# Adding six key row tiles on GpSimd ahead of the key-sum matmuls, and rearranging the mask work around the normaliser products

## The chip, the cores and the metric

The kernel runs on one core of a Trainium2 chip. The metric is the device time of one execution in microseconds (us), as the median of several runs; lower is better. One core has five engines that run their own instruction streams in order: TensorE (PE in the profile, with its weight loads listed as PEld), VectorE (DVE), ScalarE (ACT), GpSimd (POOL) and SyncE (SP), which here only issues DMA transfers. They meet at semaphores.

## The reference, cut to what matters

The program is the forward and backward pass of one block: layer norm, linear attention with 32 heads of 20 columns, a residual, a second layer norm and a gated MLP. S is 2048 rows, D is 640 columns. Only the forward attention matters here:

```python
phi = lambda t: jnp.where(t > 0, t + 1, jnp.exp(t)) + 1e-6
pq, pk = phi(q), phi(k)
kv = jnp.einsum("bhsd,bhse->bhde", pk, v)
z = jnp.einsum("bhsd->bhd", pk)                 # key sums over all 2048 rows
num = jnp.einsum("bhqd,bhde->bhqe", pq, kv)
den = jnp.einsum("bhqd,bhd->bhq", pq, z)[..., None] + 1e-6
o = num / den
```

`z` is the vector of 640 key sums. For every query row, `den` needs the products `pq * z` added up inside each head.

## The kernel before, in words

Rows are split in 16 tiles of 128 (`t` = 0 to 15), columns in 5 chunks of 128 (`m` or `c` = 0 to 4). The schedule is manual: each engine carries out its instructions in the order in which the Python code issues them, so an instruction that waits holds up everything behind it on its engine.

**The key loop (lines 515 to 558).** For each row tile, TensorE multiplies the normalised rows by the key weights (`p1_mm`, line 266), ScalarE takes exp and relu of the result (lines 293 and 294, groups `mq` and `rq`), and VectorE finishes phi in two instructions (line 297, a tensor_scalar on `mq`, and line 298, an add). They write `pk_all[:, t, :]`, bf16. VectorE's part of tile t is held back and issued in the next round of the loop (`held`, `phi_rest`). TensorE also accumulates `M = pk^T x` with `m_part` (line 416), chunk by chunk of the key columns, as rows become available. Four query tiles are computed inside the loop, the others after it. In rounds 11 to 15 the loop clears a chunk of `bd` (line 551) and calls `make_mask(t - 11)`.

**The masks (lines 198 to 206).** `make_mask(m)` builds a 0/1 pattern that keeps the columns of a row's own head. VectorE sets the chunk to one (line 201), then GpSimd runs two affine selects on it (lines 203 and 205). The masks are read by `masked` (line 211), which clears the off-head entries of `kvT_block(m)`; the result `bd` feeds `f2_wT` (line 690).

**The key sums.** For chunks 0 and 1 a column of ones appended to `x` gives them along with M (`m_end`, line 425). For chunks 2, 3 and 4 `z_late` (line 329) issues 16 row tiles times 3 chunks = 48 matmuls with a one-column right side (line 333), each with its own 128x128 weight load. ScalarE copies the three columns into `Z` (line 335), `z_diag` (line 327) puts each chunk on the diagonal of a matrix `dz`, and `z_rows` (line 339) multiplies a matrix of ones by `dz` (line 343), which spreads the key sums over all 128 partitions. ScalarE copies them to `Zb` (line 346).

**The normaliser.** `r_prod(t)` multiplies a query tile by `Zb` in two halves of 320 columns, on GpSimd for t < 8 (line 358). `r_row(t)` on VectorE sums inside the heads (line 365), adds the small constant (368), inverts (369) and scales the query tile in place (372); `r_T(t)` has the scaled tile transposed by a DMA. Two buffers for each parity of t hold the products, so the product of tile t+2 waits for the sum of tile t.

**Order behind the loop (lines 573 to 624).** The order is written out by hand: query tile 4, the rest of M's chunks 0 and 1, `z_late`, ten row tiles of M's chunk 2, `z_rows`, then query tiles, products, heads and more of M in turn. After it come `q_late`, `kv3`, `f2_wT` (line 868), whose outputs are transposed to `Wp` by DMA, and the attention output `f2_at` (line 642).

Of the kernel before, what the change touches and what calls it, by code (L numbers as in the profile page):

```python
# [9 lines left out]
P = 128  # L10
BF16 = mybir.dt.bfloat16
F32 = mybir.dt.float32
ALU = mybir.AluOpType
# [5 lines left out]
S, D, H, F = 2048, 640, 32, 1728  # L19
DH = D // H  # L20
ST, DT = S // P, D // P
# [34 lines left out]
def kernel(  # L56
# [19 lines left out]
    V, A, T, G, SY = nc.vector, nc.scalar, nc.tensor, nc.gpsimd, nc.sync  # L76
# [42 lines left out]
    ones = cp.tile([P, P], BF16, name="ones")  # L119
# [6 lines left out]
    rden = cp.tile([P, ST, H], F32, name="rden")  # L126
    bd = cp.tile([P, DT, D], BF16, name="bd")
    Zb = cp.tile([P, D], BF16, name="Zb")
# [67 lines left out]
    mask = cp.tile([P, DT, M_MAX, DH], BF16, name="mask")  # L196

    def make_mask(m):
        a, b = M_H[m]
        v = mask[:, m, 0:b - a, :]  # L200
        V.memset(v, 1.0)

        G.affine_select(out=v, in_=v, pattern=[[-DH, b - a], [0, DH]], compare_op=ALU.is_ge, fill=0.0,
                        base=m * P - a * DH, channel_multiplier=1)
        G.affine_select(out=v, in_=v, pattern=[[DH, b - a], [0, DH]], compare_op=ALU.is_gt, fill=0.0,
                        base=a * DH + DH - m * P, channel_multiplier=-1)
# [27 lines left out]
    pk_all = p1.tile([P, ST, D], BF16, name="pk_all", tag="pk")  # L234
# [16 lines left out]
    def p1_tr(t, parts=((0, DT),)):  # L251
        xn = x_sb[:, t, :]
        for a, b in parts:
            tr = ps.tile([P, DT, P], BF16, name="tr", bufs=2)
            for c in range(a, b):
                T.transpose(tr[:, c, :], xn[:, c * P:(c + 1) * P], ident[:])

            A.copy(out=pqT[:, a:b, t * P:(t + 1) * P], in_=tr[:, a:b, :])
# [13 lines left out]
    def p1_mm(t, n0, between=None, halves=None):  # L272
        acc = p1_acc() if halves is None else None
        for j in range(2):
            p1_half(acc[:, j, 0:HD] if halves is None else halves[j][:, 0:HD], t, n0 + j * HD)
            if j == 0 and between is not None:
                between()
        return acc
# [6 lines left out]
    def phi_tiles():  # L285
        return [p1.tile([P, D], BF16, name=n, bufs=3) for n in ("mq", "rq")]

    def phi(acc, dst, t, parts=None):

        mq, rq = parts or phi_tiles()  # L290
        if parts is None:
            kw = dict(scale=ln1.rs[:, t:t + 1]) if t < RAW else {}
            A.activation(two(mq[:]), acc[:, :, 0:HD], AF.Exp, **kw)
            A.activation(two(rq[:]), acc[:, :, 0:HD], AF.Relu, **kw)

        def rest():
            V.tensor_scalar(out=mq[:], in0=mq[:], scalar1=1.0, scalar2=1e-6, op0=ALU.min, op1=ALU.add)
            V.tensor_tensor(out=dst, in0=mq[:], in1=rq[:], op=ALU.add)
        held.append(rest)

    def phi_rest(keep=0):
        while len(held) > keep:
            held.pop(0)()

    pqs = {}
    hx = ph.tile([P, FT * W], BF16, name="hx", tag="H1")[:, 0:11 * D].rearrange("p (t n) -> p t n", n=D)
    pq6, mbs = hx[:, 0:6, :], hx[:, 6:10, :]

    def q_home(t):
        if t < 4 or 8 <= t < 10:  # L310
            pqs[t] = pq6[:, t if t < 4 else t - 4, :]
        elif t < 8:
            pqs[t] = pf.tile([P, D], BF16, name="pql", bufs=4)[:]
        else:
            pqs[t] = pkx[0][:, DT + t - 10, :]
# [3 lines left out]
    def q_tile(t):  # L319
        q_home(t)  # L320
        phi(p1_mm(t, 0), pqs[t], t)
# [3 lines left out]
    def z_diag(m):  # L325
        dz[m] = hx[:, 10, m * P:(m + 1) * P]
        V.tensor_scalar(out=dz[m], in0=ident[:], scalar1=Z[:, m:m + 1], scalar2=None, op0=ALU.mult)

    def z_late(ms, acc):

        for t in range(ST):
            for i, m in enumerate(ms):
                T.matmul(acc[:, i:i + 1], lhsT=pk_all[:, t, m * P:(m + 1) * P], rhs=ones[:, 0:1],
                         start=(t == 0 and i == 0), stop=(t == ST - 1), skip_group_check=True)
        A.copy(out=Z[:, ms[0]:ms[-1] + 1], in_=acc[:, 0:len(ms)])
        for m in ms:
            z_diag(m)
# [12 lines left out]
    def r_prod(t):  # L350
        for j in range(2):
            js = slice(j * HD, (j + 1) * HD)
            if t < 8:
                pr[t, j] = (p1.tile([P, HD], F32, name="pr", bufs=2) if t % 2 else
                            pf.tile([P, HD], F32, name="pr", tag="h2", bufs=2))[:]
            else:
                pr[t, j] = ps.tile([P, 512], F32, name="prp", tag="at", bufs=2)[:, 0:HD]
            (G if t < 8 else V).tensor_tensor(out=pr[t, j], in0=pqs[t][:, js], in1=Zb[:, js], op=ALU.mult)
# [16 lines left out]
    def r_T(t):  # L375
        dmaT(out=pqT[:, :, t * P:(t + 1) * P], in_=pqs[t])
# [34 lines left out]
    def m_part(m, tiles, js=(0, 1)):  # L411
        if m not in macc:
            macc[m] = [ps.tile([P, 512], F32, name="macc", tag=("m", "tr")[m % 2], bufs=2) for _ in range(2)]
        for t, j in [(t, j) for t in tiles for j in js]:
            n = HD + (m < 2) * j
            T.matmul(macc[m][j][:, 0:n], lhsT=pk_all[:, t, m * P:(m + 1) * P],  # L416
                     rhs=x_ext[:, t, j * HD:j * HD + n], start=(t == 0), stop=(t == ST - 1))
# [97 lines left out]
    for t in range(ST):  # L515
        first = None
        if t < RAW:
            first = phi_tiles()
            kh = [ps.tile([P, 512], F32, name="k0", tag="m", bufs=2) for _ in range(2)]

            def act(i, j):
                A.activation(first[i][:, j * HD:(j + 1) * HD], kh[j][:, 0:HD], (AF.Exp, AF.Relu)[i],
                             scale=ln1.rs[:, t:t + 1])

            def between():
                act(0, 0)
                p1_tr(t + 1)
                act(1, 0)
            k = p1_mm(t, D, between, kh)
            act(0, 1)  # L530
            act(1, 1)
        else:
            k = p1_mm(t, D, (lambda: p1_tr(t + 1)) if t + 1 < XT_DMA else None)
        steps = v_steps.get(t, (R,) * len(held))
        for step in steps:
            if step is R:
                held.pop(0)()
            elif step[0] in V_OPS:
                V_OPS[step[0]](step[1])
        phi(k, pk_all[:, t, :], t, first)  # L540
        for when in ("A", "B", "L"):
            for step in steps:
                if step is not R and step[0] == when:
                    p1_norm(step[1])
            if when == "A" and t in QT:
                q_tile(QT.index(t))
        if 3 <= t < 7:
            ghh_chunk(t - 3, ps.tile([P, 512], F32, name="gp", tag="m", bufs=2))
        m_part(0, M0.get(t, ()))
        if t >= 11:  # L550
            V.memset(bd[:, t - 11, :], 0.0)
            make_mask(t - 11)
        if t >= 9:
            m_part(1, [2 * (t - 9), 2 * (t - 9) + 1])
        for f, *n in outs.get(t, ()):
            f(*n)
        if t in trickle:
            trickle[t]()
# [10 lines left out]
    def r_head(t):  # L569
        r_row(t)  # L570
        r_T(t)

    q_tile(4)
    m_part(0, (13, 14, 15))
    m_end(0)
# [5 lines left out]
    for go in w13[4:]:  # L581
        go()
    z_late((2, 3, 4), big())
    m_part(2, range(10))
    z_rows(((0, 1), (2, 3, 4)), ps.tile([P, 2, 512], F32, name="bigx", tag="big", bufs=2))
    r_prod(0)
    q_tile(5)
    r_prod(1)
    m_part(2, range(10, ST))
# [1 line left out]
    dmaG(out=m_v[:, 0, :], in_=mbs[:, 0, :])  # L591
    r_head(0)
    r_prod(2)
    phi_rest()
    m_part(3, range(5))
    q_tile(6)
    r_head(1)
    r_prod(3)
    phi_rest()
    m_part(3, range(5, 11))  # L600
    q_tile(7)
    kvT_block(0, big())
    r_row(2)
    r_prod(4)
    phi_rest()
    m_part(3, range(11, ST))
    m_end(3)
# [2 lines left out]
    dmaG(out=m_v[:, 1:4, :], in_=mbs[:, 1:4, :])  # L610
    r_head(3)
    r_prod(5)
    m_part(4, range(5))
    q_tile(8)
    kvT_block(1, big())
# [301 lines left out]
    for c in range(SC):  # L917
# [9 lines left out]
        for fc in range(FT):  # L927
# [8 lines left out]
            if c == 0 and fc in (5, 7, 9, 11):  # L936
                a, b = {5: (0, 3), 7: (3, 6), 9: (6, 10), 11: (10, 13)}[fc]
# [12 lines left out]
            if c == SC - 1 and fc in (1, 2, 5, 6):  # L950
                i = (1, 2, 5, 6).index(fc)
# [66 lines left out]
    for fc in range(FT - 1):  # L1018
        b, i = divmod(fc, 4)
        if fc == FT - 2:  # L1020
            gw2_tail()
        acc = ps.tile([P, 2, 512], F32, name="gw", bufs=4)
        for j in range(2):
            for t in range(ST):
                T.matmul(acc[:, j, 0:HD], lhsT=hb[b][:, t, i * P:(i + 1) * P], rhs=g2[:, t, j * HD:(j + 1) * HD],  # L1025
                         start=(t == 0), stop=(t == ST - 1))
# [200 lines left out]
    a, b = ST - 1, ST - 2  # L1227
# [90 lines left out]
    for m, (a, b) in enumerate(M_H):  # L1318
        n = (b - a) * DH
        acc = ps.tile([P, 512], F32, name="gkvT", tag="dkv", bufs=3)  # L1320
        for c in range(DT):
            T.matmul(acc[:, 0:n], lhsT=woT[:, c, m * P:(m + 1) * P], rhs=QT[:, c, a * DH:b * DH], start=(c == 0),
                     stop=(c == DT - 1))
# [38 lines left out]
    acc = d_acc()  # L1362
    for m in range(DT):
        T.matmul(acc[:, m // 4, m % 4 * P:(m % 4 + 1) * P], lhsT=ones[:], rhs=gzd[:, m, :], start=(m % 4 == 0),
                 stop=True, skip_group_check=True)
# [3 lines left out]
    for t in range(ST):  # L1369
        c, i = divmod(t, TPC)  # L1370
        u = t // 2
        acc = d_acc()
        for j in range(2):
            for k in range(DT):
                T.matmul(acc[:, j, 0:HD], lhsT=xnT[c][:, k, i * P:(i + 1) * P], rhs=gm[:, k, j * HD:(j + 1) * HD],  # L1375
                         start=(k == 0), stop=(k == DT - 1))
# [7 lines left out]
        if t in (2, 5, 8, 11, 14):  # L1384
            n = t // 3
            acc = square(mN, gkv_b, n)
            k = (4, 0, 1, 2, 3)[n]
# [119 lines left out]
```

## Time and profile before

The median of three runs is 824.03 us (823.37 to 824.87). The profiled execution spans 821.9 us.

| Engine | Busy, us | Share of the span |
|---|---|---|
| PE | 814.4 | 99% |
| PEld (weight loads) | 522.6 | 64% |
| DVE | 453.1 | 55% |
| ACT | 325.0 | 40% |
| POOL | 133.1 | 16% |

The stretch that the change touches, by windows of the span:

| Window, us | Length | PE busy | DVE busy | ACT busy | POOL busy |
|---|---|---|---|---|---|
| 38.00 to 51.64 (key loop, rounds 11 to 15, query tile 4) | 13.64 | 13.53 | 10.39 | 9.61 | 5.59 |
| 51.64 to 57.36 (key sums, spread) | 5.72 | 5.72 | 1.63 | 2.51 | 0.33 |
| 57.36 to 78.50 (products, heads, rest of M) | 21.14 | 21.14 | 19.35 | 11.79 | 11.83 |
| 78.50 to 98.40 (`f2_wT`, `Wp`, first attention outputs) | 19.90 | 19.56 | 17.07 | 15.22 | 6.59 |
| 98.40 to 821.90 (everything else) | 723.50 | 719.33 | 373.38 | 256.04 | 99.25 |

Busy time says what an engine did, not what it cost: an engine beside TensorE costs nothing until TensorE waits for it. In the timeline each row is a start, a duration, an engine, a line, an operation and its output and inputs; rows of one line that follow each other are merged, with their count. A bracket gives the idle time of the engine ahead of it and what ended it.

### The profile page before, as it was taken

How to read it: one execution, taken by the hardware profiler on the slowest of the kernel's cores; microseconds unless marked ns; L12 is line 12 of the kernel's file. 1: busy time of each engine (PE TensorE's matmuls, PEld its weight loads, DVE VectorE, ACT ScalarE, POOL GpSimd, SP SyncE). 2: the span in 40 equal slices, each digit the busy share in tenths (PEclk: the TensorE clock that was granted, in tenths of full speed). 3: DMA queues.
4: the chain of work that ended last, by engine and by line, in shares of the span. 5: the costliest groups of instructions: out<-in, count | busy, mean ns of one | idle time of the engine just before them, and what ended most of it. 6: DMA issues, size and time to landing. Idle time of an engine off the chain costs nothing.

```text
span 821.9 us, 14179 instructions
## 1 busy us (share of the span) xinstructions
PE 814.4 (99%) x5522; PEld 522.6 (64%) x5549; DVE 453.1 (55%) x961; ACT 325.0 (40%) x609; POOL 133.1 (16%) x194
## 2 busy tenths in 40 slices
PE   8999999999999999999999999999999999999998
PEld 6677544555555555777777777767777777555554
DVE  7869887999898566300057777772681545200000
ACT  7856688665565666011122212222212334211111
POOL 2243333323223212100001111110220000000000
PEclk9999999999999999999999999999999999999999
DMA  9999889696485556999677897258984898885771
GB/s 233 254 279 227 207 234 312 196 242 157 145 213 155 166 181 162 250 241 267 195 170 179 206 204 188 70 113 178 268 216 93 164 200 181 201 199 137 165 170 38
DMA packets 320883, 157.26 MB, mean 191 GB/s; under 512 B 238704, under 2 KB 314064, under 8 KB 320816
## 3 DMA queue, kind: packets, MB, share of 16 engines
q1 hardware_dynamic: 278768, 115.54, 61.3%
q0 software_dynamic: 7328, 24.48, 8.9%
q10 hardware_dynamic: 34720, 16.34, 8.7%
q8 instruction: 43, 0.70, 0.4%
q14 instruction: 24, 0.20, 0.1%
HBM read 47.01 MB, written 51.13 MB: 119 GB/s over the span
## 4 chain that ended last, share of the span: by engine, by line
PE 94%; DVE 2%; ACT 1%; DMA 1%; issue 0%; SPq 0%; POOL 0%; DVEq 0%; ACTq 0%
PE mm L386 20%; PE job L1271 20%; PE ghn L1070 14%; PE gxn L1429 8%; PE o L833 7%; PE gw L1025 7%; PE gwo L1155 3%; PE big L266 3%; PE gr L1127 3%; PE dkv L1375 3%; PE macc L416 2%; PE at L642 2%; DMA wqkv<-in_A_wqkv_dram 1%; PE dkv L1303 1%; DVE st L147 1%; DMA Wp<-pkx 1%
## 5 line engine op out<-in xcount | busy, mean ns | idle before, releaser
L1271 PE MATMUL job<-gb,hnN 128*128 128x432 bf16 (+2 forms) x656 | 117.0, 342 | 0.0
L1070 PEld LDWEIGHTS <-ggb 128*128 128x128 bf16 x864 | 84.5, 98 | 32.8
L1271 PEld LDWEIGHTS <-hnN 128*128 128x128 bf16 x656 | 63.6, 98 | 53.4
L386 PE MATMUL mm<-pqT,w 128*128 128x512 bf16 x397 | 93.1, 379 | 0.5
L386 PEld LDWEIGHTS <-w 128*128 128x128 bf16 x540 | 52.5, 98 | 63.1 <-issue 0.8
L1275 ACT CAST obs<-job 128x432 bf16<-128x432 f32 (+3 forms) x61 | 29.3, 480 | 123.1 <-PE job L1271 123.1
L833 PE MATMUL o<-w,hhT 128*128 128x320 bf16 x448 | 67.7, 299 | 0.1
L1070 PE MATMUL ghn<-w13a,ggb 128*128 128x320 bf16 x448 | 63.5, 299 | 0.0
L1070 PE MATMUL ghn<-w13b,ggb 128*128 128x320 bf16 x416 | 61.4, 299 | 0.0
L386 PE MATMUL mm<-g2T,w2T 128*128 128x512 bf16 x227 | 58.5, 379 | 0.6
L833 PEld LDWEIGHTS <-hhT 128*128 128x128 bf16 x448 | 43.8, 98 | 23.8 <-issue 0.2
L1025 PE MATMUL gw<-g,hb 128*128 128x320 bf16 x416 | 56.8, 299 | 0.0
L1135 POOL TENSOR_TENSOR sz<-Zb,g_h 128x640 f32<-128x640 bf16 x16 | 20.2, 1260 | 198.8 <-DVE g_h L1133 107.7
L1025 PEld LDWEIGHTS <-hb 128*128 128x128 bf16 x416 | 40.6, 98 | 16.0 <-issue 0.3
L1429 PE MATMUL gxn<-wqT,gT 128*128 128x320 bf16 x320 | 48.7, 299 | 0.0
L406 ACT CAST ghh<-mm 128x512 bf16<-128x512 f32 x48 | 28.3, 590 | 44.7 <-PE mm L386 39.0
L772 ACT ACTIVATE sig<-mm 128x512 bf16<-128x512 f32 x56 | 33.9, 605 | 25.1 <-PE mm L386 21.6
L1082 ACT ACTIVATE gs<-ghn 128x640 bf16<-128x640 f32 x16 | 11.2, 703 | 78.9 <-PE ghn L1070 73.4
L386 PEld LDWEIGHTS <-w2T 128*128 128x128 bf16 x260 | 25.4, 98 | 23.3
L266 PEld LDWEIGHTS <-pqT 128*128 128x128 bf16 x320 | 30.6, 98 | 14.4 <-issue 1.7
L1429 PEld LDWEIGHTS <-gT 128*128 128x128 bf16 x320 | 31.3, 98 | 12.2
L266 PE MATMUL big<-wqkv,pqT 128*128 128x320 bf16 x250 | 38.5, 299 | 0.3
(210 smaller groups left out, 1282.3 us busy)
## 6 DMA issues: line engine op xcount, KB each, us to landing
hh_d<-hhT SPq DMA_DIRECT2D x24, 256.0 KB, 2.8
gg_d<-gate POOLq DMA_DIRECT2D x24, 256.0 KB, 4.1
gg_d<-ghh POOLq DMA_DIRECT2D x24, 256.0 KB, 3.5
ggb<-gg_d SPq DMA_DIRECT2D x6, 896.0 KB, 5.4
ggb<-gg_d ACTq DMA_DIRECT2D x6, 832.0 KB, 5.7
out_dram<-obs ACTq DMA_DIRECT2D x39, 108.0 KB, 3.0
x_sb<-in_A_x_dram SPq DMA_DIRECT2D x6, 640.0 KB, 5.4
ggb<-gg_d SPq DMA_DIRECT2D x2, 1728.0 KB, 13.5
```

The costliest lines, as they stand in the source:

```text
L266: T.matmul(acc, lhsT=pqT[:, c, t * P:(t + 1) * P], rhs=wqkv[:, c, n0:n0 + HD], start=(c == 0), stop=(c == DT - 1))
L386: T.matmul(acc[:], lhsT=w[:, c, fc * P:(fc + 1) * P], rhs=rhs[:, c, :], start=(c == 0), stop=(c == DT - 1))
L406: A.copy(out=ghh[n // 2][:, n % 2, :], in_=acc[:])
L772: A.activation(sig[:, i, :], gp[:], AF.Sigmoid)
L833: T.matmul(o2["ps"][:, 0:HD], lhsT=hhT[c][:, fc, i * P:(i + 1) * P], rhs=w2[:, fc, j * HD:(j + 1) * HD], start=(fc == 0), stop=(fc == FT - 1))
L1025: T.matmul(acc[:, j, 0:HD], lhsT=hb[b][:, t, i * P:(i + 1) * P], rhs=g2[:, t, j * HD:(j + 1) * HD], start=(t == 0), stop=(t == ST - 1))
L1070: T.matmul(acc[:, j, 0:HD], lhsT=ggb[t // 2][:, k, lo:lo + P], rhs=rhs[:, j * HD:(j + 1) * HD], start=(k == 0), stop=(k == NG - 1))
L1127: T.matmul(gr[t][:, j, 0:HD], lhsT=ghT[t][:, c, :], rhs=wT2[:, c, j * HD:(j + 1) * HD], start=(c == 0), stop=(c == DT - 1))
L1155: T.matmul(acc[m][:, j, 0:n], lhsT=r_sb[:, t, m * P:(m + 1) * P], rhs=g_hx[:, t, j * HD:j * HD + n], start=(t == 0), stop=(t == ST - 1))
L1271: T.matmul(acc[:, 0:n], lhsT=lhs[:, t, m * P:(m + 1) * P], rhs=rhs(t), start=(t == 0), stop=(t == ST - 1))
L1275: A.copy(out=ob, in_=acc[:, 0:n])
L1429: T.matmul(acc[:, j, 0:HD], lhsT=g, rhs=wqT[:, k, j * HD:(j + 1) * HD], start=(k == 0), stop=(k == 14))
```

## The change: what it does and what it is for

It has four parts.

1. *Sums on GpSimd.* In rounds 11 to 15 `z_add(t - 1)` adds up the columns 256 to 639 of the key tiles 9 to 14 in f32, five additions of 128x384, in the place where the masks were made. The accumulator `z_acc` lies in the storage of `rden`, which is not yet in use. After the last, `z_split` writes the sum as two bf16 rows: the rounded sum (`z_hi`) and what the rounding left (`z_lo`), placed in storage that `dz` and `Zb` take over later.
2. *Fewer matmuls.* `z_late` runs over the ten tiles that were not added (0 to 8 and 15) and the two rows of the split, 12 in place of 16, so 36 one-column matmuls in place of 48.
3. *The spread comes sooner.* `z_rows` and `r_prod(0)` are issued behind six row tiles of M's chunk 2 in place of ten; the other four follow.
4. *Masks later.* The five memsets on VectorE become one over the whole mask tile, behind the key loop. The affine selects of chunk 0 follow it; those of chunks 1 to 4 are issued behind `r_prod(2)` to `r_prod(5)`.

The diff, with its context cut:

```diff
     def make_mask(m):
         a, b = M_H[m]
         v = mask[:, m, 0:b - a, :]
-        V.memset(v, 1.0)
-
...
+    ZG = (9, 10, 11, 12, 13, 14)
+    z_acc = rden.rearrange("p t h -> p (t h)")[:, 0:D - 2 * P]
+    z_hi, z_lo = hx[:, 10, 2 * P:], Zb[:, 2 * P:]
+
+    def z_add(t):
+        a = pk_all[:, ZG[0], 2 * P:] if t == ZG[1] else z_acc
+        G.tensor_tensor(out=z_acc, in0=a, in1=pk_all[:, t, 2 * P:], op=ALU.add)
+
+    def z_split():
+        G.tensor_copy(out=z_hi, in_=z_acc)
+        G.tensor_tensor(out=z_lo, in0=z_acc, in1=z_hi, op=ALU.subtract)
+
     def z_late(ms, acc):
 
-        for t in range(ST):
+        rows_ = [pk_all[:, t, 2 * P:] for t in range(ST) if t not in ZG] + [z_hi, z_lo]
+        for k, row in enumerate(rows_):
             for i, m in enumerate(ms):
-                T.matmul(acc[:, i:i + 1], lhsT=pk_all[:, t, m * P:(m + 1) * P], rhs=ones[:, 0:1],
-                         start=(t == 0 and i == 0), stop=(t == ST - 1), skip_group_check=True)
+                T.matmul(acc[:, i:i + 1], lhsT=row[:, (m - 2) * P:(m - 1) * P], rhs=ones[:, 0:1],
+                         start=(k == 0 and i == 0), stop=(k == len(rows_) - 1), skip_group_check=True)
...
         if t >= 11:
             V.memset(bd[:, t - 11, :], 0.0)
-            make_mask(t - 11)
+            z_add(t - 1)
+        if t == ST - 1:
+            z_split()
         if t >= 9:
             m_part(1, [2 * (t - 9), 2 * (t - 9) + 1])
...
+    V.memset(mask[:], 1.0)
+    make_mask(0)
     q_tile(4)
     m_part(0, (13, 14, 15))
...
     z_late((2, 3, 4), big())
-    m_part(2, range(10))
+    m_part(2, range(6))
     z_rows(((0, 1), (2, 3, 4)), ps.tile([P, 2, 512], F32, name="bigx", tag="big", bufs=2))
     r_prod(0)
+    m_part(2, range(6, 10))
     q_tile(5)
     r_prod(1)
...
     r_prod(2)
+    make_mask(1)
     phi_rest()
...
     r_prod(3)
+    make_mask(2)
     phi_rest()
...
     r_prod(4)
+    make_mask(3)
     phi_rest()
...
     r_prod(5)
+    make_mask(4)
     m_part(4, range(5))
```

## The prediction

> **What bounds the kernel now.** I read the page first (PE busy 99% of the span), then the chain of work that ended last between 45 and 80 us, which shows whose work sets the time where the edit lies. Columns: start, us, what.
>
> ```profile
> 50.55 1.38 PE macc L416 x10
> 51.94 1.18 PE bigx L333 x48
> 53.12 2.77 PE macc L416 x20
> 55.88 0.28 PE bigx L343 x5
> 56.16 1.36 PE big L266 x10
> 57.52 3.02 PE macc L416 x22
> 60.54 1.36 PE big L266 x10
> ```
>
> Every piece is TensorE's and each begins where the last ends, from 38.1 to 78.9 us. TensorE has no hole here that another engine could give back. The 48 one-column matmuls hold it for 1.18 us, 24.6 ns each; six row tiles of two halves are 12 x 138 ns = 1.66 us (2.77 / 20 = 138 ns).
>
> Second, the timeline of all engines from 50 us, for slack around the sums. Columns: start, us, engine, line, operation, output and inputs, count, idle before.
>
> ```profile
> 49.74 0.49 DVE L298 TENSOR_TENSOR pk_all<-mq,rq 128x640 bf16<-128x640 bf16 x1 [0.20 <-ACT rq L294]
> 50.39 1.55 PE L416 MATMUL macc<-x_sb,pk_all 128*128 128x320 bf16 x10
> 51.78 1.34 PE L333 MATMUL bigx<-ones,pk_all 128*128 128x1 bf16 x48
> 53.15 0.24 ACT L335 COPY Z<-bigx 128x3 f32<-128x3 f32 x1
> 53.57 0.73 DVE L327 TENSOR_SCALAR hx<-ident,Z 128x128 bf16<-128x128 bf16 x4
> 55.72 0.44 PE L343 MATMUL bigx<-hx,ones 128*128 128x128 bf16 x5
> 57.03 0.79 POOL L358 TENSOR_TENSOR pr<-hx,Zb 128x320 f32<-128x320 bf16 x1 [7.67 <-ACT Zb L346]
> ```
>
> The last diagonals are ready at 54.30 and TensorE turns to them at 55.72. GpSimd idles 7.67 us until `Zb` comes. VectorE idles from 50.23 to 52.63.
>
> Third, the timeline of VectorE behind it, where GpSimd's products run beside.
>
> ```profile
> 59.78 0.97 DVE L372 TENSOR_TENSOR hx<-hx,rden 128x640 bf16<-128x640 bf16 x1
> 60.67 1.86 DVE L297 TENSOR_SCALAR mq<-mq 128x640 bf16<-128x640 bf16 x1
> 62.64 0.49 DVE L298 TENSOR_TENSOR pql<-mq,rq 128x640 bf16<-128x640 bf16 x1
> ```
>
> Line 297 takes 0.26 us alone and 1.86 us here, while `r_prod(2)` runs on GpSimd from 60.79 to 62.33. VectorE is then without a pause until 78.3, when the last `bd` mask is applied; TensorE needs `bd` for line 690 at 78.52. So VectorE is second in line, with 0.2 us in hand at that point.
>
> TensorE's only holes from 38 us to 300 us, start to start, are 0.33 us at 89.9 (the wait for `Wp`), and 0.16 and 0.24 near 96.5 (the wait for `hn`, line 160): 0.73 us. A gain is thus limited to matmuls removed plus 0.7 us.
>
> **What the Trainium skill says.** "TensorE: Matmul & The Clock Gate", "Wait — 56ns, not 53.3ns?": the spacing of small matmuls never falls below about 25 ns. The trace agrees, 24.6 ns. "SBUF — State Buffer", "SBUF: two separate sides": VectorE and GpSimd share a port pair as an exclusive lock; a VectorE operation in a two-port mode, or with two SBUF inputs against a GpSimd operation that reads SBUF, waits for the whole GpSimd instruction. The 1.86 us above agrees. "GPSIMD Engine Reference", section 3.1, prices a GpSimd tensor_tensor of 2048 f32 columns at 4497 ns, 2.2 ns a column; no tensor_tensor of that kind with wide f32 inputs is in the trace, so this is my upper price.
>
> **The change part by part.**
>
> *Fewer matmuls.* 12 x 24.6 ns = 0.30 us off TensorE, on the chain. Their weight loads go with them; TensorE was fed in time (48 loads in 1.39 us), so nothing more.
>
> *Additions on GpSimd.* Row of the trace: 320 columns, bf16 inputs, 0.79 us; 640 columns (line 1135) 1.26 us; so 1.48 ns a column and 0.31 fixed, 0.88 us for 384. With the skill's 2.2 ns a column it is 1.16. I take 1.0 us each. The inputs are written by line 298 at 41.3 (tile 10), 42.9, 45.2, 46.5 and 48.05 (tile 14); each addition ends before the next input, the last at 49.1. The split is a copy (0.6 to 0.8; estimate, one input) and a subtraction (1.0), so `z_lo` is there at about 50.8, at worst 51.6. `z_late` starts at 51.78 and reaches the split rows last, 30 matmuls in, at 52.5. No wait in the normal case, and 0.9 us in hand at worst.
>
> *What the additions do to VectorE.* They take 5 to 6 us of the shared port where two selects per round took 0.85. Lines 297 and 298 (0.26 + 0.49 us) can lose up to one addition per round. A round lasts 2.18 us on TensorE; addition, 297 and 298 need 1.0 + 0.75 = 1.75, so this fits, except round 12, with a query tile too (2.5 us), which recovers in the next. VectorE gives up five memsets of 0.175 us for it. The tight point is tile 15: written at 50.23, needed by the fifth matmul of the group at 50.39, that is 50.9, 0.7 us of slack. Behind the waiting line 297 of tile 15 only line 298, the mask memset and the first `z_diag` are queued. If 297 gets in between copy and subtraction it costs nothing; if it starves until 50.8, tile 15 comes at 51.5 and TensorE stalls 0.6 us. I take nothing, and 0.6 for the range.
>
> *One memset.* 140 columns 0.175, 160 columns 0.192: 0.85 ns a column, so 0.72 us for 800. It lies in VectorE's idle stretch 50.23 to 52.63. Free. `make_mask(0)` follows on an idle GpSimd. Free.
>
> *Earlier spread.* `z_late` ends at 52.67; 12 matmuls later is 54.33, against diagonals ready at 54.30. ScalarE is unchanged there (line 335 waits behind line 425 anyway). At most 0.1 us of stall; I take nothing. `Zb` comes 1.4 us sooner and the products start at 55.7. The order of TensorE's work changes, its amount does not, so directly this is worth nothing. VectorE gains: the first sums start 1.4 us sooner, and line 297 of query tile 5 is then issued at 59.4, ahead of `r_prod(2)`, which still waits for the DMA issue of line 591 (its source is ready at 59.8). The 1.6 us collision is gone. VectorE is some 3 us ahead at 60.2.
>
> *Masks between the products.* Four times 0.35 + 0.35 to 0.50, 0.7 to 0.85 us of GpSimd, right behind a product, where VectorE wants the port for line 372 or 297. GpSimd idled 6.1 us there, waiting for line 365, so GpSimd has the time; VectorE can lose up to 0.85 us four times, 3.4 us. The first two fall where VectorE would wait for TensorE's `kvT_block(0)` at 65 us; the last two cost up to 1.7, and it enters them about 1.2 us ahead. Net at 78.3: 1.2 us early to 0.5 us late, against 0.2 in hand. I take no stall.
>
> Sum: -0.30 us, everything else hidden. 824.03 - 0.30 = 823.7 us.
>
> **The rivals.** *(A) Likeliest, 0.66*: as above, 823.7. *(B) The lead of VectorE also closes holes behind 79 us*: with all 0.73 us it is 824.03 - 0.30 - 0.73 = 823.0. For it: `hn` waits in VectorE's queue. Against: the `Wp` wait follows ScalarE and DMA, which only shift along. 0.12; still within 0.2%. *(C) The port becomes a bound*: GpSimd runs its operations end to end and VectorE starves as at 60.67. Tile 15 late by 0.6, `bd` late by 0.5 + 0.3: 824.03 - 0.30 + 1.4 = 825.1; with two starvations of the length seen (1.6 us each) on the path, 826.9. For it: the 1.86 us row. Against: line 368, which meets the same products, takes 0.48 us at 63.95 and gets in between two of them, and there is slack at all but two points. 0.22.
>
> **How the numbers follow.** Likeliest 823.7. A gain over 0.2% is 1.65 us, more than the 1.03 us that TensorE's holes and the removed matmuls allow, so only the measurement's spread (823.4 to 824.9 before) could show it: 0.05. C beyond +1.65 us needs starvation at both tight points and more, and I know the lock only from one long row: 0.20. The rest, 0.75, within 0.2%. Range 822.7 (B less 0.3 of spread) to 825.8 (C's first figure plus 0.7 of spread).
>
> **What would show it.** Right: line 333 has 36 matmuls in 0.89 us on the chain; the chain stays on TensorE from 38 to 78 us; `Zb` at about 55.6; line 297 no longer above 1 us at 60; line 690 starts 0.3 us sooner. Wrong: TensorE waiting for `pk_all` near 50.9, for `z_lo` near 52.5, for `hx` at line 343 or for `bd` at line 690; additions above 1.2 us; masks that stretch line 372.

## The result and the profile after

The changed kernel takes 827.3 us (median of six executions, 824.5 to 827.8) against 824.1 us (823.4 to 824.9) for the kernel before on the same chip: ratio 1.0031, 95% interval [1.0016, 1.0047]. A ratio here is worked out from the single executions and is not the quotient of the two medians. The changed kernel is slower by about 3 us, and its time lies above the predicted range. Its executions fall in two groups, four at 827.2 to 827.8 with a mean granted TensorE clock of 0.998 (1.000 is the full clock) and two at 824.5 and 825.6 with 1.000. Three executions of the experiments below were far slower than all others (1068.09 us in `after_again`, 4141.73 in `late_before`, 852.44 of the kernel before beside `own_swap`) and are left out of the ratios. The profiled execution of the changed kernel is of the second group (span 823.8 us, before 821.9), so the profile shows only part of the loss.

**Around the edit, up to 80 us.** The chain of work that ended last, between 45 and 80 us of the changed kernel (start, us, what):

```profile
50.49 1.38 PE macc L427 x10
51.87 0.88 PE bigx L344 x36
52.75 1.67 PE macc L427 x12
54.42 0.28 PE bigx L354 x5
54.70 1.10 PE macc L427 x8
55.79 1.36 PE big L264 x10
57.15 3.02 PE macc L427 x22
60.17 1.36 PE big L264 x10
```

The chain stays on TensorE, as before, and the sums are 36 matmuls in 0.88 us where they were 48 in 1.18. The spread (line 354) starts at 54.42 in place of 55.88. The query tile of line 264 that began at 60.54 begins at 60.17. Counted from the first line of each chain, 50.55 and 50.49, that is 0.31 us sooner.

The timeline of all engines in the same stretch (start, us, engine, line, operation, output and inputs, count, idle before):

```profile
49.68 0.90 DVE L296 TENSOR_TENSOR pk_all<-mq,rq 128x640 bf16<-128x640 bf16 x1 [0.22 <-ACT rq L292]
50.29 0.64 POOL L336 CAST hx<-rden 128x384 bf16<-128x384 f32 x1
50.69 0.72 DVE L586 MEMSET mask<- 128x800 bf16 x1
51.02 0.92 POOL L337 TENSOR_TENSOR Zb<-rden,hx 128x384 bf16<-128x384 f32 x1
51.71 0.89 PE L344 MATMUL bigx<-ones,pk_all 128*128 128x1 bf16 x30
52.54 0.21 PE L344 MATMUL bigx<-ones,Zb 128*128 128x1 bf16 x3
53.50 0.73 DVE L325 TENSOR_SCALAR hx<-ident,Z 128x128 bf16<-128x128 bf16 x4
54.26 0.44 PE L354 MATMUL bigx<-hx,ones 128*128 128x128 bf16 x5
55.57 3.03 POOL L369 TENSOR_TENSOR pr<-hx,Zb 128x320 f32<-128x320 bf16 x4 [2.92 <-ACT Zb L357]
59.21 1.95 DVE L295 TENSOR_SCALAR mq<-mq 128x640 bf16<-128x640 bf16 x1
```

The split's second row (`Zb`, line 337) is written at 51.94 and read at 52.54. The products start at 55.57, before at 57.03, with GpSimd idle 2.92 us ahead of them in place of 7.67. Line 295 still takes 1.95 us beside the products. TensorE waits for none of this.

**Where the time went.** The waits of TensorE between 38 and 120 us (us in total, times, longest), first of the kernel before:

```profile
PE at L642 <- DMA Wp<-pkx: 0.2, 1, 0.2
```

and of the changed kernel:

```profile
PE trh L764 <- DVE hn L160: 2.7, 1, 2.7
```

The small wait for `Wp` is gone, and a long one for `hn` has come, 40 us behind the edit. (This view leaves out the smallest waits.) The chain there, in the changed kernel (start, us, what):

```profile
88.23 9.71 DMA pqT<-pql
97.94 0.03 issue
97.97 0.05 DVEq L160
98.02 0.05 issue
98.07 0.46 DVE hn L160
98.52 0.05 issue
98.57 0.81 PE trh L764 x10
99.38 7.87 PE mm L397 x36
```

`hn` of row tile 2 takes its storage from the tag of the query tiles (`tag="pql"`, `f2_hn`). It takes over the buffer of query tile 5, which the DMA transpose `r_T(5)` (line 387, `pqT<-pql`) still reads. So VectorE may not write `hn` before that transpose has landed, that is, before its completion has been signalled, and TensorE's transposes follow `hn`. The timelines of VectorE show `hn` without this wait before:

```profile
95.67 0.48 DVE L365 TENSOR_REDUCE rden<-pr 128x16 f32<-128x320 f32 x1
96.06 0.96 DVE L160 TENSOR_SCALAR hn<-x_sb,ln_mv,ln_rs 128x640 bf16<-128x640 bf16 x2
```

and with it after:

```profile
94.95 0.48 DVE L376 TENSOR_REDUCE rden<-pr 128x16 f32<-128x320 f32 x1
98.07 0.80 DVE L160 TENSOR_SCALAR hn<-x_sb,ln_mv,ln_rs 128x640 bf16<-128x640 bf16 x2 [2.64 <-DMA pqT<-pql]
```

In the kernel before, the transpose landed at 95.88 and `hn` began at 96.06, 0.18 us later. The chain above has 0.13 us from the landing to the start of `hn` where `hn` did wait, so the landing was hidden with some 0.05 us in hand. In the changed kernel VectorE is free for `hn` at 95.4 and waits 2.64 us. The issue of the transpose among the DMA issues of the kernel before (output and input, queue, operation, count, us from issue to landing):

```profile
pqT<-pql SPq DMA_TRANSPOSE x1, 6.4
```

and of the changed kernel:

```profile
pqT<-pql SPq DMA_TRANSPOSE x1, 9.7
```

SyncE's queue around it (start, us, line, operation), before:

```profile
86.94 1.28 SPq L376 DMA_TRANSPOSE pqT<-pql  x1
88.66 0.68 SPq L186 DMA_DIRECT2D x_sb<-in_A_x_dram  x1
89.45 1.25 SPq L376 DMA_TRANSPOSE pqT<-pql  x1
```

and after:

```profile
86.01 1.28 SPq L387 DMA_TRANSPOSE pqT<-pql  x1
87.74 0.38 SPq L186 DMA_DIRECT2D x_sb<-in_A_x_dram  x1
88.23 2.43 SPq L387 DMA_TRANSPOSE pqT<-pql  x1
```

The transpose is issued 1.22 us *sooner* and lands 2.06 us *later*. In the trace, the packets of GpSimd's stores `r_d`, `m_d` and `pq_d` (5120 bytes each), which are in flight at that time, took up to 2.7 us in the changed kernel, and at most 1.0 us in the kernel before. So the stores were slowed in the same stretch as the transpose.

The sum for this pair of profiled executions: 0.30 us of matmuls and 0.33 us at the `Wp` wait gained. The holes near `hn`, stretches in which TensorE starts nothing, are 2.9 us in place of 0.40 us. That is -0.63 + 2.5 = +1.9 us, the difference of the spans, 823.8 - 821.9. The rest of the loss, in the slower group of executions, is TensorE's clock, as the run `after_again` below shows.

### The profile page after: what moved, and what is told of

It reads as the page before. It is cut to its first block, busy times and chain, and to the rows that moved or that the text cites. A ratio compares the mean times of both kernels' runs of the same rounds, so it can differ in the third digit from the quotient of the medians.

```text
span 823.8 us, 14165 instructions
## 1 busy us (share of the span) xinstructions
PE 814.5 (99%) x5510; PEld 522.9 (63%) x5537; DVE 455.6 (55%) x957; ACT 325.1 (39%) x609; POOL 141.3 (17%) x201
## 4 chain that ended last, share of the span: by engine, by line
PE 96%; DMA 2%; ACT 1%; DVE 1%; issue 0%; SPq 0%; DVEq 0%
PE mm L397 20%; PE job L1291 19%; PE ghn L1090 14%; PE gxn L1449 8%; PE o L853 7%; PE gw L1045 7%; PE big L264 4%; PE gwo L1175 3%; PE macc L427 3%; PE gr L1147 3%; PE dkv L1395 3%; PE at L662 2%; DMA pqT<-pql 1%; DMA wqkv<-in_A_wqkv_dram 1%; PE dkv L1323 1%; PE gp L397 1%
```

## The experiments

None of these kernels leaves out part of the computation. The ratio is always to the kernel before in runs on the same chip. Times in a trace count from the start of its span, and two executions of one kernel can differ there: `after` and `after_again` begin the key sums at 51.71 and 52.39 us. Across traces, durations and waits are therefore safer to compare than points in time.

**Is the wait for the buffer the whole loss?** `own` gives `hn` of row tile 2 the row of `hx` that held `z_hi`, in place of a query tile's buffer. The landing of the transpose then doesn't matter to it.

```diff
-        hn[t] = (pf.tile([P, D], BF16, name="hn", tag="pql", bufs=4) if t == 2 else
+        hn[t] = (hx[:, 10, :] if t == 2 else
```

> The kernel after, with one edit: the normalised tile hn of row tile 2 (line 160) is written to a dead row of hx and no longer to a pql buffer, so it does not wait for the transpose of query tile 5 (line 387). Theory L (landing): the whole loss is this wait, 2.9 us of TensorE in the trace of after. Then the hole at 95.5 us is gone, the time is 823.0 to 823.7 us, the granted clock is 1.000 in every run, and the transpose may still land late. Rival P (port): the additions and masks cost VectorE or TensorE time elsewhere; then the time stays at 825 us or more.

Measured: 823.27 us (20 executions, 822.9 to 824.5) against 823.99, ratio 0.9991 [0.9983, 0.9998]. From the timeline of VectorE in `own`:

```profile
95.98 0.44 DVE L160 TENSOR_SCALAR hx<-x_sb,ln_mv,ln_rs 128x640 bf16<-128x640 bf16 x1
```

and of TensorE's weight loads there:

```profile
96.47 0.28 PEld L764 LDWEIGHTS <-hx 128*128 128x128 bf16 x5 [0.49 <-DVE hx L160]
96.99 0.28 PEld L764 LDWEIGHTS <-hn 128*128 128x128 bf16 x5 [0.24 <-DVE hn L160]
```

`hn` is written at 95.98, although the transpose needed 9.4 us and landed at 98.29, and the view of TensorE's waits between 38 and 120 us is empty. Only the two small holes near 96.5 us are still there, 0.16 and 0.23 us between the matmuls (the weight loads, which run ahead, idle longer), much as in the kernel before; they follow VectorE, not the DMA. The wait for the buffer, with the clock behind it, is the whole loss: with one line changed, the changed kernel is a little faster than the kernel before. The slow landing by itself costs nothing here.

The same line in the kernel before, `own_before`:

> The kernel before, with hn of row tile 2 in the dead row of hx, so that it does not wait for the transpose of query tile 5. Theory L: before loses to the same wait in some of its executions, so the tail above 825 us disappears and the median falls to 823.4 to 823.8; against the kernel after with the same edit (823.27) that leaves 0.2 to 0.5 us for what the change brings by itself. Rival: before is not touched by the wait, stays at 824.0 with its tail.

Measured: 823.58 us against 823.88, ratio 0.9990 [0.9983, 0.9997]. The tail is gone: the slowest of 20 executions took 824.3 us, while 7 of 40 of the kernel before took more than 825. So the kernel before, too, seems to lose to this wait in some of its executions, though none of those was profiled. In the trace the two small holes near 96.5 us remain (0.16 and 0.23 us), and the hole for `Wp` is not there, though nothing that bears on it was changed. Part of what `own` gains was thus there to be had before the change. By the medians, 0.72 - 0.30 = 0.4 us are left for the change, near the 0.30 us of the matmuls; by the ratios, 0.9991 and 0.9990, nothing is left. The intervals reach 0.6 us to either side, so what the change gains by itself is not settled.

**The unchanged kernel once more.** `after_again` is the changed kernel, to see how the landing and the clock vary.

> The kernel after, unchanged, for a second trace and many more executions beside those of before. Theory L: most executions at 825 to 828 us, the rest near 823.5, since the landing of the transpose of query tile 5 differs from one execution to the next; in the trace hn of row tile 2 waits for it. If the executions scatter as those of before do (median 824.0), the loss seen at first was chance.

Measured: 825.48 us (12 executions, ten of them from 824.9 to 827.4) against 823.88, ratio 1.0020 [1.0011, 1.0029]. The loss is there again, by the ratios 1.6 us where the first runs had 2.6. Its transpose took 9.1 us. The profiled execution took 827.14 us with a clock of 0.998. Busy time of the engines by stretch in it (stretch, its length, busy us and instructions of PE, PEld, DVE, ACT, POOL, then granted clock, DMA share, GB/s):

```profile
99.00:103.00 4.00, 4.00 (x18) 1.94 (x17) 3.76 (x10) 1.87 (x3) 0.00 (x0) 0.60 1.12 283
103.00:110.00 7.00, 7.00 (x35) 3.17 (x33) 4.61 (x11) 6.57 (x13) 2.39 (x4) 1.00 0.36 97
```

and in the first profiled execution of the changed kernel:

```profile
99.00:103.00 4.00, 4.00 (x24) 1.89 (x24) 3.76 (x11) 2.96 (x5) 0.00 (x0) 1.00 1.10 275
```

In the four microseconds behind the stall, the mean granted clock was 0.60, and TensorE did 18 matmuls where it did 24 with the full clock. A finer window shows it at 0.50 from 98.8 to 102.2 us. Six matmuls of 512 columns began 427 ns apart in place of 216, and with the ten transposes ahead of them the stretch took 1.6 us longer. That fits the distance between the two groups of executions: the net 1.9 us of the first profile, and another 1.6 us of clock where the granted clock is 0.998. "TensorE: Matmul & The Clock Gate", section "What's actually happening", of the Trainium skill states that the clock is halved after at least one idle window of about 3.4 us, and that these windows run on freely, whatever the kernel does. The half agrees with the 0.50 here. But the hole was only 2.3 us in this execution, 2.9 us in the one that kept its clock, and 3.7 us in `only12` below, whose clock fell to 0.50 too. So the length alone doesn't decide; whether it is the place of the hole in such a window, no run here shows.

**Which part of the change brings it?** `only12` is the kernel before with the additions and the fewer matmuls, the masks staying in the loop; `only3` has only the sooner spread; `only4` only the masks moved; `no3` is the changed kernel without the sooner spread.

```diff
# only12, against before
         if t >= 11:
             V.memset(bd[:, t - 11, :], 0.0)
+            z_add(t - 1)
+            if t == ST - 1:
+                z_split()
             make_mask(t - 11)
... (and z_late as in the change)
# only3, against before (no3 is the reverse, against after)
-    m_part(2, range(10))
+    m_part(2, range(6))
     z_rows(((0, 1), (2, 3, 4)), ps.tile([P, 2, 512], F32, name="bigx", tag="big", bufs=2))
     r_prod(0)
+    m_part(2, range(6, 10))
...
# only4, against before
-        V.memset(v, 1.0)
...
-            make_mask(t - 11)
...
+    V.memset(mask[:], 1.0)
+    make_mask(0)
...
+    make_mask(1)
```

> The kernel before with the first two parts alone: additions on GpSimd and 36 key-sum matmuls; masks and their memsets stay in the loop behind the additions. TensorE gains 0.30 us if the split rows come in time. GpSimd has 1.05 us of addition and 0.85 of selects in rounds of 2.18 us, so the split may end at 52.5, up to 0.5 us late. Theory L: 823.5 to 824.5 if the transpose lands in time, up to 826 if the 0.3 us are enough to meet it too early.

> The kernel before with the third part alone: the spread behind six row tiles. No matmul is removed, the masks stay in the loop. Theory L with the lead of VectorE as the cause: SyncE issues the transposes of Wp up to 0.9 us sooner, the one of query tile 5 collides, time 824.5 to 827. If the third part is not the cause: 823.7 to 824.1, as before.

> The kernel before with the fourth part alone: one memset over the masks, the selects behind the products. Theory O: VectorE has neither the earlier spread nor additions; the selects delay it by up to 0.85 us a product, so SyncE issues the transposes of Wp no sooner, q_out stays first: 823.7 to 824.3. If the masks between the products are what hurts (the port rival): 825 or more, with TensorE waiting for bd near 78.5 us.

> The kernel after without its third part: z_rows behind ten row tiles of M's chunk 2, as before. Theory L: VectorE loses the lead of the earlier spread (1.4 us at 57 us), SyncE issues the transposes about as in before, time 823.5 to 824.3. Rival (the lead has nothing to do with it): 825 to 827.8.

| kernel | us | before | ratio [95%] | transpose issued, us to landing | TensorE waits for `hn` |
|---|---|---|---|---|---|
| `only12` | 828.26 | 823.88 | 1.0041 [1.0026, 1.0056] | 89.66, 10.0 | 3.5 |
| `only3` | 824.60 | 823.88 | 1.0002 [0.9994, 1.0011] | 89.03, 8.3 | 1.3 |
| `only4` | 824.67 | 824.03 | 1.0005 [0.9997, 1.0014] | 91.39, 5.9 | 0.2 |
| `no3` | 825.03 | 823.99 | 1.0006 [0.9992, 1.0020] | 89.44, 7.3 | 0.9 |

Only `only3` came out in the range expected of it; `only12`, `only4` and `no3` lie above theirs. Parts 1 and 2 without the others (`only12`) lose more than the whole change. The intervals of the other three include 1, so they show no loss. In these four traces the wait for `hn` goes with the time that the transpose took, whatever the part. The waits of TensorE in `only12`:

```profile
PE trh L760 <- DVE hn L160: 3.5, 1, 3.5
PE macc L429 <- DVE pk_all L298: 0.7, 1, 0.7
```

and, from its timeline, the matmuls of M at tile 15:

```profile
51.76 1.00 PE L429 MATMUL macc<-x_sb,pk_all 128*128 128x320 bf16 x6 [0.67 <-DVE pk_all L298]
```

With the additions *and* the masks in the same rounds, VectorE is late with tile 15, and TensorE waits 0.67 us: the first step of rival C, on which the prediction put 0.6 us. Part 3 acts behind this point, so it is moving the masks (part 4) that spares the full change this wait.

**Does VectorE's lead make it?** `hold` is the changed kernel with VectorE held up for 0.85 us by three memsets of unused storage ahead of `phi_rest`, so that the transpose goes out about as late as before.

```diff
+    def hold():
+        for a, b in ((0, D), (0, D), (0, 3 * P)):
+            V.memset(hx[:, 10, a:b], 0.0)
...
-    run((q_late, 10, f2_mT), (q_late, 11, kv3), (phi_rest,),
+    run((q_late, 10, f2_mT), (q_late, 11, kv3), (hold,), (phi_rest,),
```

> The kernel after, with three dead memsets on VectorE (0.85 us in all, into a row of hx that is no longer read) between the masks of kv3 and the phi of query tile 10. They give back VectorE's lead of 0.9 us ahead of the Wp transposes, so SyncE issues the transposes of Wp and of query tiles 4 and 5 when the kernel before did. Theory L, in the form that the earlier issue is what makes the transpose of query tile 5 collide with the stores of GpSimd's queue: its landing comes back to about 6.4 us after the issue, time 823.6 to 824.3. If the landing is late for another reason: 825 to 827.8, as after.

Measured: 824.72 us against 823.99, ratio 1.0003 [0.9989, 1.0017]. The transpose went out at 89.45, as in the kernel before, and took 7.0 us. The wait for `hn` shrank to 0.3 us, and the hold itself cost 0.6 us at `wt` (line 710). The time lies between the two ranges, and 6 of 12 executions took more than 825 us. In the trace, then, holding VectorE back shortens the landing, as `no3` does by leaving out the sooner spread (7.3 us). How much of the loss the lead explains is not settled, and `only12`, which lacks the sooner spread, had the slowest transpose of the four.

**Which transfer crowds it?** `stores` moves GpSimd's stores of M and of query tiles 10 to 13 (`m_d`, `pq_d`) behind `f2_hn(3)`; `early` issues them some 4 us sooner than the changed kernel does.

```diff
# stores
-(r_store, 5, 6), (r_store, 4, 5), (f2_m_out,), (q_out, 10, 14), (load_w2T, 8 * P, 10 * P), (mlp_ghh, 4),
+(r_store, 5, 6), (r_store, 4, 5), (load_w2T, 8 * P, 10 * P), (mlp_ghh, 4),
...
-(f2_half, 4, 1, True), (f2_hn, 3),
+(f2_half, 4, 1, True), (f2_hn, 3), (f2_m_out,), (q_out, 10, 14),
...
# early
-(f2_wT, 4), (phi_rest,), (q_late, 14),
+(f2_wT, 4), (phi_rest,), (f2_m_out,), (q_out, 10, 14), (q_late, 14),
```

> The kernel after, with the two stores m_out and q_out (160 and 640 KB, GpSimd's queue) issued behind hn of row tile 3 and no longer at 88 us. Theory L, in the form that these stores take the DMA engines from the transpose of query tile 5: it lands within 7 us of its issue, ahead of 95.3 us, time 823.0 to 823.8. If the stores are not what delays it: 825 to 827.8.

> The kernel after, with m_out and q_out (GpSimd's queue) issued ahead of r_prod(7), some 4 us sooner, so that they are on their way before SyncE issues the transpose of query tile 5; hn of row tile 2 still waits for that transpose. Theory O (order): the transpose lands late when it is issued ahead of q_out and shares the DMA engines with it (after: 0.57 us ahead, landing after 9.7 us), and in time when q_out is first (before: 0.28 us behind, 6.4 us). Then it lands within 7 us, time 823.0 to 823.8. Rival (the stores have to be away from it altogether): 824.5 or more.

Measured: `stores` 823.51 us, ratio 0.9987 [0.9979, 0.9995], landing after 5.4 us and no wait for `hn`. `early` 824.25 us, ratio 0.9993 [0.9980, 1.0005], landing after 5.9 us, but outside the range set for its time; it has small holes in place of the long one (0.43 us at 93.0, and a wait for `hn` of 0.3). Without the 800 KB of these stores beside it, whether they go later or sooner, the transpose is quick. The two together with `own`, `own_early`, gave no more than `own` alone:

> The kernel after with both remedies: hn of row tile 2 in the dead row of hx, and m_out and q_out ahead of r_prod(7). Theory L: no wait for the transpose and no collision; 823.0 to 823.4, no execution above 824.5, faster than before and after.

Measured: 823.96 us, ratio 1.0000 [0.9991, 1.0009]; that is a miss. What the early stores cost was not followed up.

**Is it the order of issue?** In the kernel before, the transpose goes out after the stores (89.45, against 88.63 and 89.17); in the changed kernel, ahead of both (88.23, against 88.27 and 88.80). If a transpose that is queued ahead of the stores were the slow one, the kernel before would turn slow when its stores are held up. `late_before` puts two memsets of unused storage (GpSimd) ahead of `f2_m_out`, `late_stores_before` three of them ahead of `r_store`.

```diff
# late_before (two), late_stores_before (three)
+    def hold():
+        for _ in range(2):
+            G.memset(hx[:, 10, :], 0.0)
...
# late_before
-(r_store, 4, 5), (f2_m_out,),
+(r_store, 4, 5), (hold,), (f2_m_out,),
...
# late_stores_before
-(r_prod, 7),
+(r_prod, 7), (hold,),
```

> The kernel before, with two dead memsets on GpSimd (about 0.6 us each, into a row of hx no longer read) between r_store and m_out, so that m_out and q_out are issued behind the transpose of query tile 5, as in after. Nothing of the change is in it. Theory O: the transpose lands 8 to 10 us after its issue, hn waits, time 825 to 828. If the order is not the cause: 823.9 with the tail of before.

> The kernel before, with three dead memsets on GpSimd (about 0.6 us each, into a row of hx no longer read) ahead of the two r_store, so that all four stores of GpSimd's queue start about 1 us later and the transpose of query tile 5 is issued about 1 us behind the first of them, as in after (1.1 us), and no longer 1.95 us. Nothing of the change is in it. Theory C (coincidence): where the transpose is issued within about 1.1 us of the first r_store it jams with the stores (after, own, only3: landing after 8.3 to 9.7 us); then it lands 8 us or more after its issue and the time is 825 to 827. If the distance is not what counts: landing within 7 us, time 823.9 to 824.3.

Measured: `late_before` 824.13 us, ratio 0.9998 [0.9990, 1.0005]. The transpose went out at 89.34, ahead of both stores (89.67 and 90.20), and landed after 5.4 us, as quickly as in any of these runs: the order against `m_d` and `pq_d` alone is not the cause. `late_stores_before` 824.44 us, ratio 1.0016 [1.0003, 1.0029], with 7 of 20 executions above 826.6 us, against 2 of 23 of the kernel before. The edit did not bring the transpose as near to the first `r_store` as it was meant to: SyncE's issues came later too, and the distance in the trace is 1.72 us in place of about 1. There the transpose took 6.3 us, and TensorE waited 0.7 us for `hn`. So a loss comes in the kernel before, with nothing of the change in it, only by shifting the stores; its slow executions were not profiled, so what they waited for is not shown.

**What stands ahead of the transpose on SyncE's queue?** A load of 320 KB (`x_sb`, line 186). `swap` issues the transpose ahead of it.

```diff
-(r_T, 4), (load_x, 4, 6), (r_head, 5), (r_prod, 7),
+(r_T, 4), (r_head, 5), (load_x, 4, 6), (r_prod, 7),
```

> The kernel after, with the transpose of query tile 5 issued ahead of the 320 KB load of row tiles 4 and 5 of x on SyncE's queue (at about 87.3 us in place of 88.2). Stores and w2T as in after. If the late landing comes from queueing behind that load while the stores begin: it lands within 6 us of its issue, ahead of 93.5 us, time 823.0 to 824.0. If not: landing at 95 us or later, 825 to 828.

Measured: 823.08 us (12 executions, seven from 822.87 to 823.09) against 823.81, ratio 0.9996 [0.9987, 1.0004]. The issue of the transpose in `swap`, among the DMA issues:

```profile
pqT<-pql SPq DMA_TRANSPOSE x1, 6.9
```

and SyncE's queue there:

```profile
86.17 4.65 SPq L387 DMA_TRANSPOSE pqT<-pql  x2
90.88 1.22 SPq L186 DMA_DIRECT2D x_sb<-in_A_x_dram  x1
```

It was issued at 87.96, even sooner than in the changed kernel, took 6.9 us and landed at 94.91, later than the 93.5 that was expected; `hn` was written at 95.51, and TensorE did not wait for the transpose. So in this trace the early issue did no harm once the load stood behind it. One of the 12 executions took 826.38 us with a clock of 0.998, so the loss may not be gone from all of them.

Two other ways to move SyncE's queue told little. `sp_late` put three writes of 128 x 4 bytes to DRAM ahead of the transpose, and `w2early` took the load of `w2T` from behind it to about 77 us.

```diff
# sp_late
+    ticks = [dram.tile([P, 2], BF16, name=f"tick{n}_d") for n in range(3)]
+
+    def tick():
+        for d in ticks:
+            dma(out=d[:], in_=ones[:, 0:2])
...
-(load_x, 4, 6), (r_head, 5),
+(load_x, 4, 6), (tick,), (r_head, 5),
...
# w2early
     load_x(0, 4)
+    load_w2T(8 * P, 10 * P)
...
-(q_out, 10, 14), (load_w2T, 8 * P, 10 * P), (mlp_ghh, 4),
+(q_out, 10, 14), (mlp_ghh, 4),
```

> The kernel after, with three tiny extra transfers (128 x 4 bytes each) on SyncE's queue ahead of the transpose of query tile 5, so that it is issued about 1.2 us later, 2.3 us behind the first r_store; the stores stay. Theory C: it lands within 7.3 us of its issue, near 96 us, and the time falls to 823.8 to 824.8, the rest of the loss being a shorter wait. If the distance is not what counts: landing after 8 us or more, 825.5 to 828.

> The kernel after, with the transposing load of columns 1024 to 1279 of w2T issued at about 77 us, ahead of the transposes of Wp, and no longer at 90.7 us behind the transpose of query tile 5. Stores, hn and everything else as in after. Theory T (three streams): the transpose jams because GpSimd's stores and the w2T load are both in flight with it; then it lands within 7 us of its issue and the time is 823.0 to 824.0. If stores and the transpose jam without w2T: landing after 8 us or more, 825 to 828.

Measured: `sp_late` 836.43 us, ratio 1.0154 [1.0136, 1.0172]: the small writes themselves took 12.9 to 16.4 us to land and held up everything behind them, with a wait of 10.3 us for `hn`; too coarse a tool for the question, and a miss. `w2early` 825.08 us, ratio 1.0007 [0.9995, 1.0020]: the transpose took 6.9 us, but the earlier load shifted the issues, and TensorE waited 0.5 us for `Wp` and 1.0 us for `pqT`. The landing came out as expected and the time did not; inconclusive.

**Two remedies together.** `own_swap` is the changed kernel with the edits of `own` and `swap`.

> The kernel after with two of the remedies together: hn of row tile 2 in the dead row of hx, and the transpose of query tile 5 ahead of the x load. Theory L: nothing waits for the transpose any more, so the executions lie close together at 822.9 to 823.3 us, none above 824.5, faster than before and after. If a further wait on the same DMA engines (Wp, x) shows up, 823.3 to 824.

Measured: 823.15 us (21 executions, 822.8 to 824.3) against 823.70, ratio 0.9991 [0.9984, 0.9998]. It is faster than the kernel before by 0.5 us, and by 2 to 4 us than the changed kernel was on other chips. It is not measurably better than `own` alone, nor, by the ratios, than `own_before`, which has nothing of the change.

**What stays open.** The transpose and the packets of the stores are slow together. The longest store packet took 1.7 to 2.9 us in the five traces in which the transpose took 8.3 to 10.0 us (`after`, `after_again`, `own`, `only3`, `only12`). In the traces with 5.4 to 7.3 us it took 1.0 us or less, but for `w2early` (1.5). Removing the stores, or the load ahead, or the lead brought both down, each in one or two traces. Why these packets take so long, and what in the timing decides it, is not settled. Nor was it tested whether work of VectorE and GpSimd, which move along with the transfers, has a part in it. The distance between the first of `r_store` and the transpose only tends to tell, where stores and load are as in the changed kernel: issued up to 1.1 us after it, the transpose took 8.3 to 9.7 us (`after`, `after_again`, `own`, `only3`), from 1.95 us on, 5.4 to 7.3; but between the two lie `hold` (7.0), `late_stores_before` (6.3) and `only12` (10.0).

## Why the prediction was wrong

**Fewer matmuls**: right. 36 matmuls in 0.88 us, predicted 0.89; the 0.30 us are gained.

**Additions and split**: right in price, late in time. GpSimd's additions took 1.05 to 1.14 us, except one of 0.91, near the 1.0 taken and within the upper price of 1.16. But the last ended at 50.22, not 49.1: line 296 of VectorE took about 1.0 us beside three of the additions, in place of 0.49, and tile 14 was written at 48.94 in place of 48.05. The prediction had allowed for such a delay and left it out of these times. `z_lo` was there at 51.94, past the "at worst 51.6" of the text, and still 0.6 us before its use. Tile 15 came at 50.58, in time, so nothing was lost there; the risk named for it was real, as `only12` shows.

**Memset and earlier spread**: right. 0.72 us in VectorE's idle stretch; the spread at 54.42 with less than 0.1 us of stall; products at 55.57, predicted 55.7.

**The collision of line 297 (now 295)**: wrong, at no cost. I had it issued ahead of the products and cleared; it came at 59.21, ahead of the two products that began at 59.34, and still took 1.95 us. The prediction had read the 1.86 us before as the wait for one GpSimd instruction; a product takes 0.79 us, so the 1.6 us of waiting are two. VectorE had gained enough elsewhere: line 710 started at 78.14, or 0.31 us sooner, counted from the start of the key sums (predicted 0.3).

**Masks between the products**: right. `bd` was masked by 77.36, and TensorE didn't wait for it.

**"everything else hidden"** is the step that failed. The sum stopped at 79 us, where VectorE and TensorE come out sooner, and rival B took the lead to be either harmless or a gain: "For it: `hn` waits in VectorE's queue. Against: the `Wp` wait follows ScalarE and DMA, which only shift along." The first is true of the kernel before and leaves out what comes next: the two small holes do follow VectorE's queue, for they stay where `hn` has its own storage (`own`, `own_before`), but `hn` also needs a buffer that a DMA releases, and that had 0.05 us in hand. The term for this wait was put at nothing; it measured 2.5 us of TensorE. The second sentence is wrong: "only shift along" is what a transfer need not do when it moves against others that stay. This one went from 6.4 to 9.7 us. (The `Wp` wait is gone in the trace of the changed kernel, whose `Wp` transposes went out 0.9 us sooner, 79.48 in place of 80.38; but it is gone in `own_before` too, so the change is not shown to have closed it.) Why the transpose then takes longer stays open. Behind the wait came the clock, up to 1.6 us, of which the forecast had nothing. Ahead of it the sum held: in this pair of traces TensorE was 0.7 us ahead of the kernel before at 94.8 us, about what rival B counts to there (0.30 + 0.33).

**Rival C**, the only one on the slower side, foresaw a loss for another reason. The port took nothing from TensorE in the full change; C's 825.1 to 826.9 us come near the measured time by accident.

## What to carry to other kernels

A small wait ahead of an instruction deserves to be followed to everything that releases it, including the storage that it writes into: a shared buffer ties it to the last reader, here a DMA, and a margin of 0.05 us is no margin when an edit moves the engines by 0.7. An edit that lets an engine run ahead moves the issue of transfers, and a transfer that is moved may land later than it did; list the transfers that will be in flight beside it. When TensorE bounds the kernel and stalls for some two microseconds, as here, look at its clock behind the stall as well.

## What the runs showed that was not expected

- The same SBUF transpose of 128x640 bf16 took 5.4 to 10.0 us from issue to landing (13.2 in `sp_late`), with different transfers in flight beside it; the five `Wp` transposes of the changed kernel between 79 and 86 us, which met no stores, took 2.6 us (median).
- A stall of 2.3 us was followed in `after_again` by a mean granted clock of 0.60 over 4 us and cost TensorE another 1.6 us, while a stall of 2.9 us in the other profiled execution was not.
- Three writes of 128 x 4 bytes to DRAM (`sp_late`) took 12.9 to 16.4 us to land, in a kernel that was 12.8 us slower than the kernel before.
- A VectorE operation of 0.26 us alone (line 295) took 1.95 us beside GpSimd's products, through two of them, though it was issued 0.13 us ahead of the first.
